# One core, RWKV attention into balanced experts: the threshold search on whole 16-bit distances, with its digits in partitions and its digit counts added up in PSUM

## The chip, the cores and the metric

One Trainium2 chip, one of its cores. The time is the device time of one execution, in microseconds (us); the kernel before has a median of 393.06 us over 3 runs (392.99 to 393.11).

## What is computed

The reference is an RWKV attention over `r, k, v` of 4 batches x 8 heads x 768 steps x 48 channels, whose output is regarded as 3072 tokens of 384 channels, and then a mixture of 8 experts with exactly balanced loads:

```python
logits = x @ w_gate                      # 3072 x 8
order = np.argsort(-logits.flatten())
for idx in order:                        # greedy, highest score first
    tok, e = idx // E, idx % E
    if assigned[tok] >= 0 or counts[e] >= cap:
        continue                         # cap = 3072 // 8 = 384
    assigned[tok] = e
    counts[e] += 1
for e in range(E):
    mask = assigned == e
    out[mask] = np.maximum(x[mask] @ w1[e], 0.0) @ w2[e]
```

`w1` is 384 x 1024 for each expert and `w2` 1024 x 384. The greedy loop can be done expert by expert: every free token proposes to its best open expert; the first expert that reaches 384 proposals, as a threshold on the score comes down, is full and closes with the tokens above the threshold, and the rest goes on without it. So seven searches for a threshold come one after another, and each also gives the 384 token numbers of one expert.

## The kernel before

It has three stretches. The **attention** (class `Mild`) fills about the first 125 us and writes the token rows to DRAM and the scores to `LG` (128 partitions x 24 tokens x 8 experts; called `ML` in the class `Assignment`). The **bridge** (to about 163 us) is written by hand under a fixed order: one expert, the "star", has its first 256 tokens (`EARLY`) chosen while attention still runs, and the matmuls of these (`x.early`, called piece by piece through `go(m)`) are laid between the steps of searches one and two. Then come the **experts** (`x.run`), whose matmuls are seven-product and fifteen-product schemes on half-size blocks (L1656, L1753, L1784) beside plain ones (L1679, L1811). There a scheduler orders the work: searches three to seven are a generator `later()`, and `due` in `x.run` pulls its next step at set parts of an expert's own work; the last argument of `x.run`, `{1: 5, 2: 7, 3: 8, 4: 8, 5: 7}`, says how many steps are pulled beside which expert.

A **search** is `likely_steps` (L1079). `m` (L1088) is each token's best open score, `prop` says which expert that is. Three times it divides the interval of thresholds by 16: `count` (L968 to L991) makes `ind` (128 partitions x 24 tokens x 16 candidate thresholds, 1 where the token's score reaches it), and three matmuls multiply it with `prop` (L980), eight tokens each, into `counts`. Of that 128x64 block only the diagonal of 8 blocks means anything, so VectorE (DVE) masks it (`own`), adds it up (`cnt`, L988), spreads the result over 16 digits (`wide`), and a fourth matmul with a matrix of ones (L991) gives every partition the 16 x 8 counts. From these DVE gets the digit `dg`, the next `cand` and `low` (L1103 to L1114); after the third digit also `fills`, `fmax` (the expert that closes) and `acc` (its tokens, L1132). Two matmuls (L1136, L1137) and a scan number the tokens; `tokens` then lists them (matmuls L1441, L1466), and GpSimd (POOL) gathers the rows with three indirect DMAs `xg` (L1557). `yield`s stand behind each count, each sum and the numbering, seven in a search.

`leave` (L1068 to L1073) closes the expert and the tokens: DVE builds a mask `dead` and a predicated copy puts a large negative number (`NEG`) into `LG`; POOL adds `acc` to `taken` and `fmax` to `last`. Before, `taken` is read only by the step for the last expert.

```python
tt(ind, self.by_token(m, ND), self.by_expert(cand), ALU.is_ge)                 # L968
tt(self.own[:, 0:G, :], each, self.same, ALU.mult)
nc.tensor.matmul(all_ps..., self.ones_h, wide..., start=True, stop=True)       # L991
nc.vector.copy_predicated(out=self.ML, mask=dead, data=self.neg...)            # L1071
```

Of the kernel before, what the change touches and what calls it, by code (L numbers as in the profile page):

```python
# [737 lines left out]
class Assignment:  # L738
# [24 lines left out]
    def __init__(self, ctx, tc, ML, CAP, C):  # L763
# [34 lines left out]
        new("digit_of_e", [128, ND, E], F16)  # L798
        new("digits", [128, ND], I32)
# [5 lines left out]
        new("cells", [128, 3, ND])  # L805
        new("cell", [128, 3])
# [20 lines left out]
    def constants(self):  # L827
# [39 lines left out]
        Q, NC = 128 // LO, self.CAP // 128  # L867
        nc.gpsimd.memset(self.quarter, 1.0)
        yield
        for sign, base in ((1, 0), (-1, LO - 1)):  # L870
# [10 lines left out]
        own = self.pool.tile([128, 2], I32, name="own_parts", bufs=1)  # L881
# [8 lines left out]
        yield  # L890
        nc.vector.tensor_scalar(out=self.turn, in0=self.iota[:, 0:Q], scalar1=self.own_turn, scalar2=None,
# [7 lines left out]
                                op0=ALU.mult, op1=ALU.add)  # L899
        yield  # L900
# [41 lines left out]
    def guess(self, ps, ident):  # L942

        nc, ND, most = self.nc, self.ND, self.most
        with ExitStack() as part:
            pool = part.enter_context(self.tc.tile_pool(name="guess", bufs=1))
            nc.tensor.matmul(ps, most.to_broadcast([128, 128]), ident, start=True, stop=True)
            nc.vector.tensor_reduce(out=self.value, in_=ps, axis=AX.X, op=ALU.max)
            nc.vector.tensor_single_scalar(out=self.value, in_=self.value, scalar=0.25, op=ALU.mult)
            rel = pool.tile([128, 3, ND], F32, name="rel")  # L950
            nc.vector.tensor_scalar(out=rel[:, 0, :], in0=self.digits, scalar1=1.0 / ND, scalar2=-1.0,
                                    op0=ALU.mult, op1=ALU.add)
            nc.vector.tensor_single_scalar(out=rel[:, 1, :], in_=self.digits, scalar=ND ** -2.0, op=ALU.mult)
            nc.vector.tensor_scalar(out=rel[:, 2, :], in0=self.digits, scalar1=-1.0, scalar2=ND ** -3.0,
                                    op0=ALU.add, op1=ALU.mult)
            nc.vector.tensor_scalar(out=self.cells, in0=rel, scalar1=self.value, scalar2=None, op0=ALU.mult)
            for g in range(3):
                nc.vector.tensor_single_scalar(out=self.cell[:, g:g + 1], in_=self.value,
                                               scalar=float(ND) ** -(g + 1), op=ALU.mult)
# [83 lines left out]
    def general_fill(self):  # L1043

        out = self.new_outs()
        with ExitStack() as part:
            pool = part.enter_context(self.tc.tile_pool(name="surely", bufs=1))
            self.surely(pool, **out)
        tok = self.tokens(out["place"])
        self.leave(out)  # L1050
        return out["fmax"], tok
# [10 lines left out]
    def leave(self, out):  # L1062

# [15 lines left out]
    def likely_steps(self, fmax, acc, place, on_fmax=None):  # L1079
        nc, ML, pool, ps, tt = self.nc, self.ML, self.pool, self.ps, self.tt  # L1080
        NT, E, ND, CAP = self.NT, self.E, self.ND, self.CAP
# [6 lines left out]
        nc.vector.tensor_reduce(out=m, in_=ML, axis=AX.X, op=ALU.max)  # L1088
# [3 lines left out]
        nc.vector.scalar_tensor_tensor(out=low, in0=self.cell[:, 0:1], scalar=float(-ND), in1=start,  # L1092
                                       op0=ALU.mult, op1=ALU.add)
        for g in range(3):
            all_ps = yield from self.count(pool, m, prop, cand, self.digit_of_e)
            if g == 0:
                eq = pool.tile([128, NT, E], F32, name="eq", bufs=1)
                tt(eq, prop, self.by_expert(self.first_e), ALU.mult)
                em = pool.tile([128, NT], F32, name="em")
                nc.vector.tensor_reduce(out=em, in_=eq, axis=AX.X, op=ALU.max)  # L1100
            if g < 2:
                base = pool.tile([128, ND], F32, name="base")
                nc.vector.tensor_scalar(out=base, in0=self.cells[:, g + 1, :], scalar1=low, scalar2=None, op0=ALU.add)  # L1103
                most = pool.tile([128, ND], F32, name="most")
                nc.vector.tensor_reduce(out=most, in_=all_ps, axis=AX.X, op=ALU.max)
                full = pool.tile([128, ND], F32, name="full")
                nc.vector.tensor_single_scalar(out=full, in_=most, scalar=float(CAP), op=ALU.is_ge)
                dg = pool.tile([128, 1], F32, name="dg")
                nc.vector.tensor_reduce(out=dg, in_=full, axis=AX.X, op=ALU.add)
                cand = pool.tile([128, ND], F32, name="cand")  # L1110
                nc.vector.scalar_tensor_tensor(out=cand, in0=self.cell[:, g:g + 1].to_broadcast([128, ND]), scalar=dg,
                                               in1=base, op0=ALU.mult, op1=ALU.add)
                was, low = low, pool.tile([128, 1], F32, name="low")
# [980 lines left out]
```

## Time and profile before

| | |
|---|---|
| median of the runs | 393.06 us |
| the profiled execution, its own time | 391.89 us |
| its span, from the first instruction to the last | 389.9 us |
| granted TensorE clock | 0.995 |
| TensorE (PE) busy | 371.9 us, 95% |
| VectorE (DVE) busy | 276.8 us, 71% |
| ScalarE (ACT) busy | 206.2 us, 53% |
| GpSimd (POOL) busy | 144.1 us, 37% |

In a row of the timeline stand the start, the time from the first start to the last end, the engine, the line, the operation with out<-in, for a matmul the tile of the array it uses (rows*columns), its shape and how many in a row; in brackets the idle time before it and what ended that. Ends of matmuls are modelled and overlap the next start, so what a matmul costs PE is read from start to start. An fp32 matmul is listed as two.

### The profile page before, as it was taken

The page shows a single profiled execution, that of the slowest core. Times are in us where ns is not written, and L with a number is a line of the kernel's source. Part 1 is how long each engine was busy: PE and PEld are TensorE (multiplying, and loading weights), DVE is VectorE, ACT ScalarE, POOL GpSimd, SP SyncE. Part 2 cuts the span into 40 slices and gives each one's busy share as a digit, 9 for nine tenths or more (in the row PEclk, how much of TensorE's full clock was granted, in tenths as well). Part 3 has the DMA queues.
Part 4 walks back from the last instruction along what each step waited for, and adds up shares of the span by engine and source line. Part 5 has one row for each costly group of instructions (what it writes and reads, how often), then busy time and mean ns, then how long its engine had stood idle before and what let it go on. Part 6 is the DMA issues. An engine that isn't in the chain of part 4 may idle for free. (4 is left out here: it accounts for less than half of the span.)

```text
span 389.9 us, 9804 instructions
## 1 busy us (share of the span) xinstructions
PE 371.9 (95%) x3720; PEld 301.0 (77%) x3720; DVE 276.8 (71%) x913; ACT 206.2 (53%) x545; POOL 144.1 (37%) x195
## 2 busy tenths in 40 slices
PE   8899999999999999999999999999999989989992
PEld 7777888888877766687577798558657779989991
DVE  6755768586885767977869939917867897994630
ACT  4897989888873311227228345423622734834620
POOL 7878979767742013022122121220330213070020
PEclk9999999999999999999999999999999999999998
DMA  7979878787593165551460470380190137190010
GB/s 146 198 151 206 194 171 178 158 179 163 108 361 83 44 218 206 185 202 43 184 220 22 148 276 23 92 334 0 49 381 16 41 130 275 34 356 20 2 62 27
DMA packets 95336, 57.36 MB, mean 147 GB/s; under 512 B 77232, under 2 KB 89520, under 8 KB 95280
## 3 DMA queue, kind: packets, MB, share of 16 engines
q1 hardware_dynamic: 91936, 47.21, 42.9%
q0 software_dynamic: 3104, 9.44, 6.8%
q8 instruction: 31, 0.51, 0.6%
q14 instruction: 25, 0.20, 0.2%
q10 hardware_dynamic: 240, 0.00, 0.0%
HBM read 47.20 MB, written 9.44 MB: 145 GB/s over the span
## 5 line engine op out<-in xcount | busy, mean ns | idle before, releaser
L1679 PE MATMUL h_ps<-xT,w 128*128 128x384 f32 (+1 forms) x264 | 71.3, 424 | 0.0
L496 ACT ACTIVATE AT<-ident,dd 128x128 f32<-128x128 f32 x192 | 59.7, 394 | 1.5 <-DVE dd L449 1.4
L1679 PEld LDWEIGHTS h_ps<-xT,w 128*128 128x128 f32 x264 | 42.8, 191 | 20.9 <-issue 0.8
L1805 POOL DMA_INDIRECT out_dram<-o_all,to x16 | 20.1, 1259 | 99.7 <-DVE cnt L988 26.0
L1557 POOL DMA_INDIRECT xg<-x_rows,tok x22 | 22.1, 1003 | 72.5 <-DVE parts L968 33.4
L1593 ACT COPY xT<-xq 32x288 f32<-32x288 f32 (+1 forms) x112 | 45.5, 406 | 3.4 <-DVE xq L1586 1.5
L1682 ACT ACTIVATE hid<-h_ps 128x384 f32<-128x384 f32 (+1 forms) x40 | 17.9, 447 | 53.4 <-PE h_ps L1679 49.9
L513 DVE COPY_PREDICATED AT<-mask,g_ps 64x512 f32<-64x512 uint8 (+1 forms) x48 | 32.4, 725 | 16.8 <-PE g_ps L506 14.5
L1811 PE MATMUL o_ps<-w,hid 128*128 128x384 f32 x96 | 34.5, 494 | 0.0
L506 PE MATMUL g_ps<-rT,kT 48*64 48x128 f32 (+1 forms) x768 | 26.3, 255 | 1.4 <-DVE AT L513 1.0
L437 POOL TENSOR_TENSOR kss<-krs,wk 128x384 f32<-128x384 f32 x24 | 24.4, 1016 | 8.1 <-DVE krs L341 4.6
L546 PE MATMUL y_ps<-AT,vts 128*64 128x128 f32 x384 | 25.7, 276 | 0.0
L444 POOL TENSOR_TENSOR rk<-rk,u_bc 128x384 f32<-128x384 f32 x24 | 24.1, 1004 | 1.9
L506 PEld LDWEIGHTS g_ps<-rT,kT 48*64 48x64 f32 x768 | 20.6, 132 | 5.1 <-issue 1.0
L443 POOL TENSOR_TENSOR rk<-krs 128x384 f32<-128x384 f32 x24 | 24.5, 1022 | 0.0
L1811 PEld LDWEIGHTS o_ps<-w,hid 128*128 128x128 f32 x96 | 17.1, 190 | 9.0 <-issue 1.5
L546 PEld LDWEIGHTS y_ps<-AT,vts 128*64 128x64 f32 x384 | 20.6, 137 | 1.0 <-issue 0.7
L1644 ACT ACTIVATE hid<-kept_P 128x384 f32<-128x384 f32 x18 | 9.4, 523 | 16.9 <-DVE kept_P L1648 16.5
L478 DVE TENSOR_TENSOR rT<-rT_ps,WR 112x512 f32<-112x512 f32 x23 | 15.7, 683 | 3.2 <-PE rT_ps L459 3.1
L565 ACT COPY x<-y_ps 128x512 f32<-128x512 f32 x24 | 14.1, 587 | 5.6 <-PE y_ps L546 4.5
L449 DVE TENSOR_REDUCE dd<-rk 128x8 f32<-128x384 f32 x24 | 13.0, 543 | 5.1 <-POOL rk L444 5.1
L459 PE MATMUL rT_ps<-ident,krs 128*112 128x128 f32 x96 | 15.7, 285 | 0.6 <-ACT krs L345 0.5
(351 smaller groups left out, 831.9 us busy)
## 6 DMA issues: line engine op xcount, KB each, us to landing
w<-in_moe_w_dram SPq DMA_DIRECT2D x18, 1536.0 KB, 9.1
krs<-in_k_dram SPq DMA_DIRECT2D x24, 192.0 KB, 3.6
krs<-in_r_dram SPq DMA_DIRECT2D x24, 192.0 KB, 3.6
vts<-in_v_dram SPq DMA_DIRECT2D x24, 192.0 KB, 3.7
x_rows<-xr SPq DMA_DIRECT2D x24, 192.0 KB, 2.7
xg<-x_rows,tok POOLq DMA_INDIRECT x22, 5.6
out_dram<-o_all,to POOLq DMA_INDIRECT x16, 2.8
out_dram<-o_sb,to POOLq DMA_INDIRECT x5, 6.3
```

The costliest lines, as they stand in the source:

```text
L437: self.nc.gpsimd.tensor_mul(self.kss[:, n % self.NS].rearrange("p (g h) d -> p g h d", g=2)[:, :, :, 0:D], src, self.wk.rearrange("p (g h) ...
L443: nc.gpsimd.tensor_mul(rk, self.krs[:, n % self.NK, 1, 0:H, 0:D], self.krs[:, n % self.NK, 0, 0:H, 0:D])
L444: nc.gpsimd.tensor_mul(rk, rk, self.u_bc)
L496: nc.scalar.mul(AT[:, z, a, :], self.ident, dd[:, h:h + 1])
L506: nc.tensor.matmul(g_ps[ts(i, PD), z, a, i * PD:], kT[rows, a, ts(i, PD)], rT[rows, a, i * PD:], start=True, stop=True)
L513: nc.vector.copy_predicated(out=AT[keys, :, :, steps], mask=mask, data=g_ps[keys, :, :, steps])
L546: nc.tensor.matmul(yv[q * PD:(q + 1) * PD, o // 2, o % 2, :], lhsT, rhs, start=(o // 2, q) not in seen, stop=stop, skip_group_check=True)
L1557: nc.gpsimd.indirect_dma_start(out=xg[:, c, :], out_offset=None, in_=x_dram[0:within, :], in_offset=bass.IndirectOffsetOnAxis(ap=tok[:, 0, ...
L1593: nc.scalar.copy(to[ts(q, 32), 0:nb, :, g, :], xq[ts(g, 32), 0:nb, :, q, :])
L1679: nc.tensor.matmul(h_ps[j][:, at], w1[:, f, ts(j, 128)], xT[:, f, at], start=(f == 0), stop=(f == KD - 1))
L1805: nc.gpsimd.indirect_dma_start(out=to, out_offset=bass.IndirectOffsetOnAxis(ap=tok, axis=0), in_=o_sb, in_offset=None)
L1811: nc.tensor.matmul(o_ps, hid[:, j, ts(c, 128)], w2[:, j, :], start=(j == 0), stop=(j == KF - 1))
```

## The change

- **Tables.** `own_slot`, `own_digit`, `same_slot`, `digit_cols`, `weight_of`, `step_of`, `first_e_h` are built with the other constants during attention (10 more steps, DVE and POOL).
- **Whole distances.** A search first works out `rel`: each token's distance below the start, in the smallest steps of the search, as int16 (L1127 to L1131). `m` gets `taken` times `NEG` added here (L1127), so a taken token drops out in `m` and not in `LG`. `ind` compares int16 with a constant table and is fp16.
- **Sums on PE, digits in partitions.** `per_slot` masks the counts, and a matmul with `digit_cols` (16 output rows, 72 columns, L1153) adds up the eight diagonal blocks with digits in 16 partitions. DVE reduces 16x72 to 16x8 (`cnt`), and decides `full`.
- **The digit, added up in PSUM.** A matmul of `weight_of` (16 rows) with `full` (one column, L1173) adds this digit, times 256, 16 or 1, to a column `digits` that every partition then reads; after the third digit another one of nine columns (L1172) gives `found`. `now` (L1143) is `rel` less the digits so far.
- **Leaving.** `leave` adds `NEG` to the column of the expert that closes. `early` no longer masks `LG` for its tokens.
- **Steps.** A search has ten `yield`s in place of seven, and the lists in the bridge and at `x.run` are adapted.

```diff
+        new("same_slot", [128, G, E])
+        new("digit_cols", [128, ND], F16)
+        new("weight_of", [ND, 3, 128], F16)
+        new("step_of", [128, 3, ND, 128 // self.LO], I16)
+        new("per_slot", [128, G + 1, E], F16)
...
+        nc.vector.tensor_scalar(out=self.same_slot, in0=self.iota[:, 0:G].unsqueeze(2).to_broadcast([128, G, E]),
+                                scalar1=self.own_slot, scalar2=None, op0=ALU.is_equal)
+        yield
+        nc.vector.tensor_scalar(out=self.digit_cols, in0=self.iota[:, 0:ND], scalar1=self.own_digit, scalar2=None,
+                                op0=ALU.is_equal)
+        yield
+        for g in range(3):
+            nc.gpsimd.memset(self.weight_of[:, g, :], float(ND ** (2 - g)))
+            yield
+            nc.gpsimd.iota(self.step_of[:, g], pattern=[[ND ** (2 - g), ND], [0, Q]],
+                           base=-ND ** 3 + (ND ** (2 - g) if g < 2 else 0), channel_multiplier=0)
+            yield
...
     def guess(self, ps, ident):
 
         nc, ND, most = self.nc, self.ND, self.most
...
+        nc.tensor.matmul(ps, most.to_broadcast([128, 128]), ident, start=True, stop=True)
+        nc.vector.tensor_reduce(out=self.value, in_=ps, axis=AX.X, op=ALU.max)
+        nc.vector.tensor_scalar(out=self.value, in0=self.value, scalar1=0.25, scalar2=1e-30, op0=ALU.mult, op1=ALU.max)
+        nc.vector.tensor_copy(self.span, self.value)
+        nc.vector.tensor_single_scalar(out=self.cell, in_=self.value, scalar=float(ND) ** -3, op=ALU.mult)
+        nc.vector.reciprocal(self.per_cell, self.cell)
...
     def leave(self, out):
+
+        nc, pool, tt = self.nc, self.pool, self.tt
+        fmax, acc = out["fmax"], out["acc"]
+        fe = pool.tile([128, self.E], F32, name="fe")
+        nc.vector.tensor_scalar(out=fe, in0=self.first_e, scalar1=fmax, scalar2=NEG, op0=ALU.is_equal, op1=ALU.mult)
+        tt(self.ML, self.ML, self.by_expert(fe), ALU.add)
+        nc.gpsimd.tensor_tensor(out=self.taken, in0=self.taken, in1=acc, op=ALU.add)
+        nc.gpsimd.tensor_tensor(out=self.last, in0=self.last, in1=fmax, op=ALU.add)
+
+    def leave_surely(self, out):
...
         i, self.fill = self.fill, self.fill + 1
         start, value, fills, upto = self.value, self.values[:, i:i + 1], self.fills[:, i, :], self.upto[:, ds(E - 2 - i, NT)]
         self.value = value
-        cand = pool.tile([128, ND], F32, name="cand")
-        nc.vector.tensor_scalar(out=cand, in0=self.cells[:, 0, :], scalar1=start, scalar2=None, op0=ALU.add)
+        low = pool.tile([128, 1], F32, name="low")
+        tt(low, start, self.span, ALU.subtract)
         m = pool.tile([128, NT], F32, name="m")
         nc.vector.tensor_reduce(out=m, in_=ML, axis=AX.X, op=ALU.max)
-        prop = pool.tile([128, NT, E], BF16, name="prop")
+        nc.vector.scalar_tensor_tensor(out=m, in0=self.taken, scalar=NEG, in1=m, op0=ALU.mult, op1=ALU.add)
+        off = pool.tile([128, NT], F32, name="off")
+        nc.vector.tensor_scalar(out=off, in0=m, scalar1=low, scalar2=start, op0=ALU.max, op1=ALU.subtract)
+        rel = pool.tile([128, NT], I16, name="rel")
+        nc.vector.tensor_scalar(out=rel, in0=off, scalar1=self.per_cell, scalar2=0.0, op0=ALU.mult, op1=ALU.min)
+        prop = pool.tile([128, NT, E], F16, name="prop")
         tt(prop, ML, self.by_token(m), ALU.is_equal)
-        low = pool.tile([128, 1], F32, name="low")
-        nc.vector.scalar_tensor_tensor(out=low, in0=self.cell[:, 0:1], scalar=float(-ND), in1=start,
-                                       op0=ALU.mult, op1=ALU.add)
+        bank = ps.tile([128, 512], F32, name="counts")
+        at = 3 * (2 * G + 1) * E
+        digits, found = bank[:, at:at + 1], bank[:, at + 1:at + 2 + E]
         for g in range(3):
-            all_ps = yield from self.count(pool, m, prop, cand, self.digit_of_e)
+            each = bank[:, ds(g * G * E, G * E)]
+            sums = bank[0:ND, ds(3 * G * E + g * (G + 1) * E, (G + 1) * E)]
+            now = rel
+            if g:
+                now = pool.tile([128, NT], I16, name="now")
+                nc.vector.tensor_scalar(out=now, in0=rel, scalar1=digits, scalar2=None, op0=ALU.subtract)
+            ind = pool.tile([128, NT // Q, ND, Q], F16, name="ind", bufs=1)
+            tt(ind, self.by_four(now, NT, ND), self.step_of[:, g].unsqueeze(1).to_broadcast([128, NT // Q, ND, Q]),
+               ALU.is_ge)
+            for j in range(NT // G):
+                nc.tensor.matmul(each, ind[:, ts(j, G // Q)].rearrange("p j d i -> p (j d i)"),
+                                 prop[:, ts(j, G), :].rearrange("p i e -> p (i e)"),
+                                 start=(g == 0 and j == 0), stop=(j == NT // G - 1), skip_group_check=True)
+            yield
+            tt(self.per_slot[:, 0:G, :], each.rearrange("p (i e) -> p i e", e=E), self.same_slot, ALU.mult)
+            nc.tensor.matmul(sums, self.digit_cols, self.per_slot.rearrange("p i e -> p (i e)"),
+                             start=False, stop=True, skip_group_check=True)
+            yield
             if g == 0:
-                eq = pool.tile([128, NT, E], F32, name="eq", bufs=1)
-                tt(eq, prop, self.by_expert(self.first_e), ALU.mult)
+                eq = pool.tile([128, NT, E], F16, name="eq", bufs=1)
+                tt(eq, prop, self.by_expert(self.first_e_h), ALU.mult)
                 em = pool.tile([128, NT], F32, name="em")
                 nc.vector.tensor_reduce(out=em, in_=eq, axis=AX.X, op=ALU.max)
+            cnt = pool.tile([ND, E], F32, name="cnt")
+            nc.vector.tensor_reduce(out=cnt, in_=sums.rearrange("p (i e) -> p e i", e=E), axis=AX.X, op=ALU.add)
+            full = pool.tile([ND, E + 1], F16, name="full")
             if g < 2:
...
-        nc.vector.scalar_tensor_tensor(out=fills, in0=dge, scalar=dg, in1=self.first_e,
+                most = pool.tile([ND, 1], F32, name="most")
+                nc.vector.tensor_reduce(out=most, in_=cnt, axis=AX.X, op=ALU.max)
+                nc.vector.tensor_single_scalar(out=full[:, E:E + 1], in_=most, scalar=float(CAP), op=ALU.is_ge)
+            else:
+                nc.vector.tensor_single_scalar(out=full[:, 0:E], in_=cnt, scalar=float(CAP), op=ALU.is_ge)
+                with nc.allow_low_precision(reason="whole numbers"):
+                    nc.vector.tensor_reduce(out=full[:, E:E + 1], in_=full[:, 0:E], axis=AX.X, op=ALU.max)
+                nc.tensor.matmul(found, self.weight_of[:, 2, :], full, start=False, stop=True, skip_group_check=True)
+            nc.tensor.matmul(digits, self.weight_of[:, g, :], full[:, E:E + 1], start=False, stop=True,
+                             skip_group_check=True)
+            yield
+
+        nc.vector.scalar_tensor_tensor(out=fills, in0=found[:, 0:E], scalar=found[:, E:E + 1], in1=self.first_e,
                                        op0=ALU.is_equal, op1=ALU.mult)
+        nc.vector.tensor_reduce(out=fmax, in_=fills, axis=AX.X, op=ALU.max)
         past = pool.tile([128, NT], F32, name="past")
-        nc.vector.tensor_scalar(out=past, in0=m, scalar1=value, scalar2=None, op0=ALU.is_ge)
-        nc.vector.tensor_reduce(out=fmax, in_=fills, axis=AX.X, op=ALU.max)
+        nc.vector.tensor_scalar(out=past, in0=rel, scalar1=digits, scalar2=-1.0 - ND ** 3, op0=ALU.subtract, op1=ALU.is_ge)
+        nc.vector.scalar_tensor_tensor(out=value, in0=digits, scalar=self.cell, in1=low, op0=ALU.mult, op1=ALU.add)
         nc.vector.scalar_tensor_tensor(out=acc, in0=em, scalar=fmax, in1=past, op0=ALU.is_equal, op1=ALU.mult)
...
-        dead = pool.tile([128, KB, E], U8, name="e_dead", bufs=1)
-        nc.vector.tensor_copy(dead, acc.unsqueeze(2).to_broadcast([128, KB, E]))
-        nc.vector.copy_predicated(out=ML[:, 0:KB, :], mask=dead,
-                                  data=self.neg.unsqueeze(2).to_broadcast([128, KB, E]))
         tt(self.taken[:, 0:KB], self.taken[:, 0:KB], acc, ALU.add)
-        nc.vector.tensor_scalar(out=self.own[:, self.G, :], in0=self.first_e, scalar1=self.star,
+        nc.vector.tensor_scalar(out=self.per_slot[:, self.G, :], in0=self.first_e, scalar1=self.star,
                                 scalar2=float(EARLY // self.G), op0=ALU.is_equal, op1=ALU.mult)
...
                 search = walk.likely_steps(**first, on_fmax=lambda fmax: have.update(v=x.load_weights(1, fmax)))
-                for m in (1, 5, 2, 5, 2, 6, 5):
+                for m in (2, 2, 2, 2, 2, 2, 2, 2, 3, 5):
                     next(search)
...
                 go(7)
+                next(search)
+                go(2)
                 next(search)
                 go(2)
                 next(search)
...
         x.run(ahead, later(), (a for a in [*out_rows[2:NT - 1], None]),
-              {1: 5, 2: 7, 3: 8, 4: 8, 5: 7}, xT)
+              {1: 7, 2: 10, 3: 11, 4: 11, 5: 10}, xT)
```

A digit of the third search beside the first expert's products, on PE. Before:

```order
L1753 MATMUL pa_ps<-w_2788,hid 128x192 x4
L980 LDWEIGHTS ind
L980 MATMUL counts<-prop,ind 128x64
L1753 MATMUL pc_ps<-w_2788,hid 128x192 x4
L1753 MATMUL pb_ps<-T_3116,S_3149 128x192 x4
L991 LDWEIGHTS ones_h
L991 MATMUL counts<-wide,ones_h 128x128
L1753 MATMUL pa_ps<-T_3118,S_3151 128x192 x4
```

Now (`per_slot`, `digit_cols`: the sums; `full`, `weight_of`: the digit):

```order
L1148 LDWEIGHTS ind
L1148 MATMUL counts<-prop,ind 128x64
L1800 MATMUL pa_ps<-w_2778,hid 128x192 x4
L1153 LDWEIGHTS digit_cols
L1153 MATMUL counts<-per_slot,digit_cols 16x72
L1800 MATMUL pc_ps<-w_2778,hid 128x192 x4
L1800 MATMUL pb_ps<-T_3089,S_3140 128x192 x4
L1173 LDWEIGHTS weight_of
L1173 MATMUL counts<-full,weight_of 128x1
L1800 MATMUL pa_ps<-T_3091,S_3142 128x192 x4
```

The stream of products is now left twice after each count and not once, both times for a small matmul. (The three counts read alike; one is shown.)

The start of the second search in the bridge, on DVE, before:

```order
L1068 TENSOR_SCALAR fe<-first_e,fmax 128x8
L968 TENSOR_TENSOR dead<-acc,fe 128x192
L1071 COPY_PREDICATED LG<-dead,neg 128x192
...
L1088 TENSOR_REDUCE m<-LG 128x24
L968 TENSOR_TENSOR prop<-LG,m 128x192
L1092 SCALAR_TENSOR_TENSOR low<-cell,values 128x1
L968 TENSOR_TENSOR ind<-m,cand 128x384
```

and now:

```order
L1094 TENSOR_SCALAR fe<-first_e,fmax 128x8
L995 TENSOR_TENSOR LG<-LG,fe 128x192
...
L1126 TENSOR_REDUCE m<-LG 128x24
L1127 SCALAR_TENSOR_TENSOR m<-taken,m 128x24
L1129 TENSOR_SCALAR off<-m,low,values 128x24
L1131 TENSOR_SCALAR rel<-off,per_cell 128x24
L995 TENSOR_TENSOR prop<-LG,m 128x192
L995 TENSOR_TENSOR ind<-rel,step_of 128x384
```

The new second row on `m` reads `taken`, which POOL writes; on POOL the order is as it was:

```order
L1604 DMA xg<-x_rows,tok 128x384
L1604 DMA xg<-x_rows,tok 128x384 x2
L1096 TENSOR_TENSOR taken<-taken,acc 128x24
L1097 TENSOR_TENSOR last<-last,fmax 128x1
L1852 DMA out_dram<-e_o_sb,to 3072x384
```

Nothing moved on POOL, but a row of DVE's search now needs one of its results, which stands behind three gathers.

More of the change, by code (lines that the diff above doesn't have):

```diff
@@ L803, in __init__ @@
         new("last", [128, 1])
-        new("cells", [128, 3, ND])
-        new("cell", [128, 3])
+        new("span", [128, 1])
+        new("cell", [128, 1])
+        new("per_cell", [128, 1])
         new("value", [128, 1])
@@ L867, in constants @@
         Q, NC = 128 // LO, self.CAP // 128
+        assert Q == 4 and G == 8 and ND == 16
         nc.gpsimd.memset(self.quarter, 1.0)
@@ L880, in constants @@
         yield
-        own = self.pool.tile([128, 2], I32, name="own_parts", bufs=1)
+        own = self.pool.tile([128, 5], I32, name="own_parts", bufs=1)
         nc.vector.tensor_single_scalar(out=own[:, 0:1], in_=self.own_i, scalar=Q.bit_length() - 1,
@@ L944, in guess @@
         nc, ND, most = self.nc, self.ND, self.most
[L945 to L951, printed above, removed]
-                                    op0=ALU.mult, op1=ALU.add)
[L953 to L959, printed above, removed]
+        nc.tensor.matmul(ps, most.to_broadcast([128, 128]), ident, start=True, stop=True)
[4 more added lines that the diff above has]
+        nc.vector.reciprocal(self.per_cell, self.cell)
     def by_token(self, t, n=None):
@@ L1049, in general_fill @@
         tok = self.tokens(out["place"])
-        self.leave(out)
+        self.leave_surely(out)
         return out["fmax"], tok
@@ L1101, in likely_steps @@
+            nc.vector.tensor_reduce(out=cnt, in_=sums.rearrange("p (i e) -> p e i", e=E), axis=AX.X, op=ALU.add)
+            full = pool.tile([ND, E + 1], F16, name="full")
             if g < 2:
[L1102 to L1112, printed above, removed]
@@ L1113, in likely_steps @@
-                was, low = low, pool.tile([128, 1], F32, name="low")
-                nc.vector.scalar_tensor_tensor(out=low, in0=self.cell[:, g:g + 1], scalar=dg, in1=was,
-                                               op0=ALU.mult, op1=ALU.add)
-        full = pool.tile([128, ND, E], F32, name="full_e")
-        nc.vector.tensor_single_scalar(out=full, in_=all_ps, scalar=float(CAP), op=ALU.is_ge)
-        dge = pool.tile([128, E], F32, name="dge")
-        nc.vector.tensor_reduce(out=dge, in_=full.rearrange("p d e -> p e d"), axis=AX.X, op=ALU.add)
@@ L1121, in likely_steps @@
-        dg = pool.tile([128, 1], F32, name="dg")
-        nc.vector.tensor_reduce(out=dg, in_=dge, axis=AX.X, op=ALU.max)
-        past_low = pool.tile([128, 1], F32, name="past_low")
-        tt(past_low, low, self.cell[:, 2:3], ALU.subtract)
-        nc.vector.scalar_tensor_tensor(out=value, in0=self.cell[:, 2:3], scalar=dg, in1=past_low,
-                                       op0=ALU.mult, op1=ALU.add)
-        nc.vector.scalar_tensor_tensor(out=fills, in0=dge, scalar=dg, in1=self.first_e,
+                most = pool.tile([ND, 1], F32, name="most")
```

21 lines of the change are left out of this document (19 added, 2 removed).

## The prediction

> **What bounds the kernel now.** I read the page's engine totals first, then busy time by stretch, then the timeline of PE beside the searches.
>
> ```profile
> PE 371.9 (95%) x3720; PEld 301.0 (77%) x3720; DVE 276.8 (71%) x913; ACT 206.2 (53%) x545; POOL 144.1 (37%) x195
> 126.00:163.00 37.00, 35.67 (x195) 25.50 (x194) 27.86 (x130) 9.42 (x23) 5.83 (x9) 1.00 0.43 146
> 163.00:383.00 220.00, 216.12 (x1214) 172.53 (x1212) 160.67 (x544) 96.75 (x228) 46.38 (x50) 1.00 0.38 134
> ```
>
> The columns of the two stretches are length, then busy time of PE, weight loads, DVE, ACT, POOL. The changed code runs in the bridge (126 to 163) and beside the experts (163 to 383). PE is idle for 37.00 - 35.67 = 1.3 us in the first and 220.00 - 216.12 = 3.9 us in the second. DVE has 160.67 of 220 us to do, so it has slack on the whole. The rule for what follows: a microsecond of extra PE work in these stretches is a microsecond at the end, and work taken from DVE is worth no more than those of the 5.2 idle microseconds that end on a search.
>
> How the searches stand in PE's stream (here the sixth search's first digit):
>
> ```profile
> 300.93 1.46 PE L1753 MATMUL pa_ps<-T,S 128*128 128x192 f32 x8
> 302.23 0.81 PE L1753 MATMUL pb_ps<-w,S 128*128 128x192 f32 x4
> 303.11 0.26 PE L980 MATMUL counts<-prop,ind 128*128 128x64 bf16 x3
> 303.21 0.90 PE L1753 MATMUL pb_ps<-w,S 128*128 128x192 f32 x4
> 303.94 1.14 PE L1753 MATMUL pa_ps<-T,S 128*128 128x192 f32 x6
> 305.07 0.22 PE L991 MATMUL counts<-wide,ones_h 128*128 128x128 f16 x1
> 305.13 0.54 PE L1753 MATMUL pa_ps<-T,S 128*128 128x192 f32 x2
> 305.50 0.81 PE L1811 MATMUL o_ps<-w,hid 128*128 128x384 f32 x2
> ```
>
> Undisturbed, eight 192-column products take 302.23 - 300.93 = 1.30 us, 0.1625 each. From 303.11 to 303.94 three counts and four products (0.65) take 0.83: the counts cost 0.18. From 305.07 to 305.50 the sum and two products (0.325) take 0.43: one lone small matmul costs 0.105, of which only 0.06 lies before the next start and 0.045 appears in the product behind it. All matmuls here use the 128*128 tile.
>
> **The change, part by part.** *DVE.* The groups of DVE from 122 us on (count | sum in us, mean in ns):
>
> ```profile
> L968 DVE TENSOR_TENSOR ind<-m,cand 128x384 bf16<-128x384 f32 x21 | 11.6, 551 | 0.0
> L968 DVE TENSOR_TENSOR wide<-digit_of_e,cnt 128x128 f16<-128x128 f16 x21 | 4.7, 223 | 0.5
> L968 DVE TENSOR_TENSOR row<-lo_of,lo 128x768 f16<-128x768 int16 x8 | 4.4, 550 | 0.0
> L968 DVE TENSOR_TENSOR oh<-hi_of,hi 128x288 f16<-128x288 int16 x7 | 2.1, 301 | 0.0
> L1071 DVE COPY_PREDICATED_SCALAR LG<-dead,neg 128x192 f32 x7 | 3.0, 424 | 0.0
> L1130 DVE TENSOR_SCALAR past<-m,values 128x24 f32<-128x24 f32 x7 | 1.6, 232 | 0.0
> ```
>
> The new `ind` reads int16 and writes fp16, as `oh` and `row` do; a line through these two (301 at 288, 550 at 768) gives 0.35 us at 384, 0.20 less than now. `wide` goes (0.22), three times in a search, and a predicated copy of 0.42 becomes an add. Five operations on 24 columns come in (`m` with `taken`, `off`, `rel`, two `now`), 0.23 each by `past`. Three times 0.20 and 0.22 against five times 0.23 is about even; with the mask, the `base`, `cand`, `low` and `dg` groups and `full_e` that also go, I estimate 2 to 3 us less per search. That DVE work is covered by PE's products now, so it is worth only the waits below. The ten new table steps run during attention, beside a PE that is the busiest engine there too: nothing.
>
> *More interruptions of PE.* Per search the three sums stay lone matmuls and three digits come in, the last of them with a second one behind it. Three times 0.105, and 0.03 for the second of a pair (313.92 to 313.95 below), is 0.345; for seven searches **+2.4 us**. Bounds: if a lone one with few rows or columns costs only those 0.03, seven of them (0.21) stand against today's three sums (0.315), -0.7 in all; if each new one costs as much as three counts, (3 x 0.18 + 0.03) x 7 = +4.0. I take the middle one, from the same kind of place and size.
>
> *Smaller tiles.* The new sums have 16 output rows, the digits are summed over 16 rows. In the attention part, weights of fewer rows or columns are listed with a smaller tile, and there changing tiles shows a price:
>
> ```profile
> 119.42 0.19 PE L1441 MATMUL e_some_ps<-e_vals,e_row 128*128 128x32 f16 x1
> 119.55 1.09 PE L546 MATMUL y_ps<-AT,vts 128*64 128x128 f32 x16
> 120.66 0.57 PE L597 MATMUL x_ps<-ident,x 112*128 112x112 f32 x4
> 121.07 0.18 PE L1466 MATMUL list_ps<-e_both,alike 128*128 128x24 f16 x1
> 121.10 0.58 PE L597 MATMUL x_ps<-ident,x 112*128 112x112 f32 x4
> 121.61 0.67 PE L546 MATMUL y_ps<-rT,states 48*64 48x128 f32 x16
> ```
>
> Four `x_ps` take 0.41 (120.66 to 121.07) when a full-size tile follows and 0.51 (121.10 to 121.61) when a 48*64 one does: 0.10 for leaving a stream of fp32. A small 16-bit matmul with a 128*64 one behind it holds PE for 0.13 (119.42 to 119.55), while between equal tiles the like takes 0.02 (313.95 to 313.97 below): 0.11 for going on in another tile. Together 0.21 for a switch out and back; of each side 0.045 is already in the 0.105 above, so 0.12 comes on top. Six switched places in a search (three sums, three digits, the pair counting once) times seven searches is 42: **+5.0 us**. Bounds: nothing, if 16 rows in the midst of 128 are no change of tile to the array; 42 x 0.21 = +8.8, if both sides are paid in full. I take the value between, which is nearer to the rows.
>
> The Trainium skill, on the page "TensorEngine Tiling (Array Packing)", section "Tiling Modes" (Key Properties), speaks against the change: "Changing tiling mode (not just tile) drains the TensorE". The 0.10 and 0.11 above agree with it. It has no price; if it didn't hold for these shapes, the sum would lose its 5.0 us.
>
> *The bridge.* The second search's `m` now waits for `taken`:
>
> ```profile
> 146.32 0.95 POOL L1557 DMA_INDIRECT xg<-x_rows,tok  x1 [0.30 <-DVE to L1484]
> 147.28 0.33 POOL L1072 TENSOR_TENSOR taken<-taken,acc 128x24 f32<-128x24 f32 x1
> 146.22 0.35 DVE L1088 TENSOR_REDUCE m<-LG 128x24 f32<-128x192 f32 x1
> 146.60 0.36 DVE L968 TENSOR_TENSOR prop<-LG,m 128x192 bf16<-128x192 f32 x1
> 142.92 4.76 PE L1932 MATMUL e_o_ps<-w,e_hid 128*128 128x384 f32 x14
> 147.59 0.26 PE L980 MATMUL counts<-prop,ind 128*128 128x64 bf16 x3
> 149.83 0.55 PE L1572 MATMUL xT_ps<-ident,xg 128*128 128x128 f32 x3 [0.55 <-DMA xg<-x_rows,tok]
> 153.31 0.22 PE L991 MATMUL counts<-wide,ones_h 128*128 128x128 f16 x1 [0.36 <-DVE wide L968]
> ```
>
> `taken` is the third gather's successor on POOL and ends at 147.61. Behind the waiting row on DVE stand `off`, `rel`, `prop`, `ind`; PE waits for these. Three times 0.23, 0.36 for `prop` and 0.35 for `ind` put the counts at 147.61 + 1.40 = 149.0. PE's cover, the same seven output products, is used up at 147.5: a new wait of about 1.5 us, where now there is none of note. Two smaller ones: the first search has three more rows of 0.23 ahead of a 0.20 shorter `ind` (about +0.4), and the second digit's sum stands straight behind its counts, with no product between, so it waits for `per_slot` (about +0.4). The later start takes away the gather's 0.55, and the shorter chain the 0.36. Together 1.5 + 0.8 - 0.9 = 1.4; some of it falls into PE's other short gaps, and I take **+1.2 us**. Bounds +0.3 (only the two small ones, less a wait) and +2.3 (nothing taken away).
>
> *Waits that go.* The waits of PE for a search beside the experts, and the largest that is not one:
>
> ```profile
> 215.13 0.22 PE L991 MATMUL counts<-wide,ones_h 128*128 128x128 f16 x1 [0.36 <-DVE wide L968]
> 217.96 0.17 PE L1136 MATMUL st_ps<-acc,ones 128*128 128x24 bf16 x1 [0.30 <-DVE acc L1132]
> 313.92 0.17 PE L1136 MATMUL st_ps<-acc,ones 128*128 128x24 bf16 x1 [0.40 <-DVE acc L1132]
> 313.95 0.17 PE L1137 MATMUL st_ps<-acc,rest_of 128*128 128x24 bf16 x1
> 313.97 1.22 PE L1656 MATMUL hc_ps<-xT,w 128*128 128x192 f32 x6
> 315.87 0.18 PE L1395 MATMUL st_ps<-sel,ones 128*128 128x48 bf16 x1 [0.67 <-DVE is_star L968]
> 351.01 0.92 PE L1656 MATMUL h_ps<-xT,w 128*128 128x192 f32 x4 [1.36 <-DVE kept_P L1648]
> ```
>
> The first two, 313.92 and 315.87 add up to 1.73 us, and the idle 3.9 less the 1.36 at 351.01, which is behind sums of products and stays, leaves 2.5 for all waits of the searches. The chain from counts to `acc` gets shorter and stands behind the same products, and `taken` now comes ahead of the scatter that holds `sel` up. I take **-2.0 us**, the four and part of the rest; bounds 0 (other DVE rows are in the way as before) and -2.5.
>
> *The sum:* 2.4 + 5.0 + 1.2 - 2.0 = +6.6 us. The profiled execution took 391.89, which becomes 398.5; the median of the runs stands 1.17 above that execution, so I predict **399.7 us**. All lower bounds give -2.9 (390.2), all upper ones +15.1 (408.2).
>
> **The rivals.** *(a) Tiles cost nothing.* The array takes 16 rows or columns like any small matmul; against it are the 0.10 and 0.11, for it that those rows come from long streams of other tiles and not from one lone matmul. 2.4 + 1.2 - 2.0 = +1.6: 394.7.
>
> *(b) The other side: faster.* The small matmuls are as cheap as the second of a pair, 0.03, since 16-column weights and one-column data leave no trace in the product behind, and tiles cost nothing; then the shorter DVE chain decides, at the waits quoted last. It gives -0.7 + 0.3 - 2.5 = -2.9: 390.2. It decides from a price of a new place, switch included, under 0.09 us: the 0.345 per search of the interruptions are three new places and one pair, and 42 places at 0.09, and seven seconds of a pair at 0.03, less the 21 sums of now at 0.105, are 1.8, which is about what the waits less the bridge give back (2.0 to 2.5, less 0.3 to 1.2). For it speaks that PE's idle time ends mostly on DVE; against it that even a 128-column lone sum costs 0.105 with no change of tile.
>
> *(c) Switches paid in full,* 0.21: 2.4 + 8.8 + 1.2 - 2.0 = +10.4: 403.5. It needs both drains on top of the interruption.
>
> *(d) The change doesn't find the right threshold:* with the distance rounded to whole steps a count might never be exactly 384, and the arm for unforeseen inputs would run attention anew, over 125 us more. The smallest step is a 4096th of the span, as before; I give it 0.01.
>
> **How the numbers follow.** Forecast 0.56, (a) 0.22, (b) 0.14, (c) 0.07, (d) 0.01. A measurement of this kernel can tell about 0.2% (0.8 us) from no change. Faster: nearly all of (b) and a little of (a), 0.15. Same: 0.06 of (a), some of (b) and of the forecast's lower edge, 0.11. Slower: the rest, 0.74. The likeliest case alone reaches from 396.5 to 402; the range goes down far enough to take in (a) and the upper part of (b), 392.0, and up to just short of (c), 402.8, which leaves out about 0.2.
>
> **What would show it.** In the changed profile: from the row of a lone sum or digit to the row behind the next products, 0.23 us more than the products take (0.105 and 0.12), and a tile other than 128*128 in its row; a wait of 1.0 to 1.5 us on PE at the second search's first counts, named after DVE, with DVE's `m` row starting when POOL's `taken` ends; no wait of PE for `acc` over 0.2 us beside the experts; PE busy in the expert stretch about 5 x 0.345 + 30 x 0.12 = 5.3 us more (five of the seven searches lie there). I am wrong if the switched rows are no dearer than 0.105 (then (a) or (b)), or if the bridge gets no longer.

## The result, and the profile after

The changed kernel takes 399.81 us (median; 399.49 to 400.01), the kernel before 393.02 us, four runs each: a ratio of 1.0172, 95% interval 1.0160 to 1.0184. It is 6.8 us slower; 399.7 us was predicted.

The page of the changed kernel, its span and engine totals, and then the two stretches of the prediction (length, busy time of PE, weight loads, DVE, ACT, POOL):

```profile
span 398.0 us, 9792 instructions
PE 380.4 (96%) x3748; PEld 303.3 (76%) x3748; DVE 258.5 (65%) x845; ACT 206.1 (52%) x545; POOL 144.1 (36%) x201
126.00:163.00 37.00, 34.78 (x196) 24.37 (x196) 18.74 (x95) 8.43 (x21) 5.60 (x9) 1.00 0.35 127
163.00:383.00 220.00, 218.10 (x1213) 171.48 (x1212) 151.79 (x509) 96.43 (x226) 44.28 (x49) 1.00 0.38 135
```

DVE lost 276.8 - 258.5 = 18.3 us of work, 2.6 us a search, as estimated, and the end came later all the same: PE gained 8.5 us of busy time for 28 more matmuls.

Where it went can be seen in one digit, the third search's first, beside the first expert's products:

```profile
174.40 0.25 PE L1148 MATMUL counts<-prop,ind 128*128 128x64 f16 x3
174.48 1.55 PE L1800 MATMUL pa_ps<-w,hid 128*128 128x192 f32 x8
175.96 0.20 PE L1153 MATMUL counts<-per_slot,digit_cols 128*16 128x72 f16 x1
176.09 1.57 PE L1800 MATMUL pc_ps<-w,hid 128*128 128x192 f32 x8
177.49 1.46 PE L1800 MATMUL pb_ps<-T,S 128*128 128x192 f32 x8
178.89 0.17 PE L1173 MATMUL counts<-full,weight_of 16*128 16x1 f16 x1
178.99 1.57 PE L1800 MATMUL pa_ps<-T,S 128*128 128x192 f32 x8
180.40 0.81 PE L1800 MATMUL pb_ps<-w,S 128*128 128x192 f32 x4
```

Eight undisturbed products take 1.30 us. The eight ahead of the digit take 178.89 - 177.49 = 1.40, the digit's own row 0.10, and the eight behind it 180.40 - 178.99 = 1.41: a matmul of one column holds PE for 0.31 us. The sum at 175.96 costs as much: 0.09 ahead (1.48, less 1.30, less the 0.09 that three counts leave behind), 0.13 itself, 0.10 behind. The tile columns read 128*16 and 16*128, where every other row here has 128*128. No engine is named in brackets: this is no wait, and the page's idle times don't show it.

In the bridge the new wait stands where it was expected. PE, POOL and DVE rows:

```profile
144.43 4.76 PE L1979 MATMUL e_o_ps<-w,e_hid 128*128 128x384 f32 x14
150.44 0.26 PE L1148 MATMUL counts<-prop,ind 128*128 128x64 f16 x3 [1.25 <-DVE ind L995]
153.73 0.55 PE L1619 MATMUL xT_ps<-ident,xg 128*128 128x128 f32 x3
156.63 0.19 PE L1153 MATMUL counts<-per_slot,digit_cols 128*16 128x72 f16 x1 [0.32 <-DVE per_slot L995]
148.79 0.24 POOL L1096 TENSOR_TENSOR taken<-taken,acc 128x24 f32<-128x24 f32 x1
149.06 0.18 DVE L1127 SCALAR_TENSOR_TENSOR m<-taken,m 128x24 f32<-128x24 f32 x1 [1.51 <-POOL taken L1096]
```

DVE's row waits 1.51 us for `taken`, PE 1.25 for the rows behind it. Against that, these are the largest of PE's bracketed waits from 126 us on, before and then after (sum, times, longest):

```profile
PE h_ps L1656 <- DVE kept_P L1648: 1.4, 1, 1.4
PE counts L991 <- DVE wide L968: 0.7, 2, 0.4
PE st_ps L1136 <- DVE acc L1132: 0.7, 2, 0.4
PE st_ps L1395 <- DVE is_star L968: 0.7, 1, 0.7
PE pa_ps L1753 <- ACT kept_P L1758: 0.6, 2, 0.4
```

```profile
PE counts L1148 <- DVE ind L995: 1.7, 2, 1.3
PE h_ps L1703 <- DVE kept_P L1695: 1.4, 1, 1.4
PE some_ps L1488 <- DVE vals L995: 0.5, 1, 0.5
PE counts L1153 <- DVE per_slot L995: 0.3, 1, 0.3
```

All four waits for a search beside the experts are gone (one of the two for `wide`, both for `acc`, and `is_star`), and so are those of products for ACT's `kept_P`. One new wait for a search has come there: 0.50 us for `vals`, at 227.77, ahead of the matmuls that list a search's tokens. The two for `ind` stand in the bridge, at the first counts of search one (0.41) and of search two (1.25).

**A ledger.** Both kernels issue the same 1245 product matmuls after attention. From the first transpose of the bridge (`e_xT_ps`) to the start of the last matmul I sum, start to start, what these take undisturbed (0.162 us for 192 columns, 0.323 for 384, 0.216 for 256, 0.112 for 128: 236.0 us in each kernel), and what each search matmul adds to the products around it (the commonest value of each kind); the rest are waits. The split between the last two rows is good to about 0.2 us, since it hangs on how the commonest value is taken.

| us | before | after | difference |
|---|---|---|---|
| the stretch | 256.1 | 263.1 | +7.0 |
| undisturbed products | 236.0 | 236.0 | 0 |
| search matmuls | 10.3 | 21.3 | +11.0 |
| waits | 9.8 | 5.8 | -4.0 |

The prices of one place: three counts 0.17, a lone sum 0.113 before and 0.328 after, a digit 0.303, the pair of the third digit 0.325, the numbering pair 0.136. The other 1.1 us by which the two spans differ lies in attention (the bridge starts at 126.41 before and 127.52 after). The runs show no steady effect of the change there: in the eleven experiments that keep its attention code and build its tables (some of them wider) the bridge starts anywhere from 125.96 to 127.47.

### The profile page after: what moved, and what is told of

It reads as the page before. It is cut to its first block, busy times and chain, and to the rows that moved or that the text cites. A ratio compares the mean times of both kernels' runs of the same rounds, so it can differ in the third digit from the quotient of the medians.

```text
span 398.0 us, 9792 instructions
## 1 busy us (share of the span) xinstructions
PE 380.4 (96%) x3748; PEld 303.3 (76%) x3748; DVE 258.5 (65%) x845; ACT 206.1 (52%) x545; POOL 144.1 (36%) x201
## 4 chain that ended last, share of the span: by engine, by line
PE 72%; issue 8%; DVE 7%; ACT 4%; DMA 3%; POOL 2%; another core or an unknown queue 1%; POOLq 0%; SPq 0%; DVEq 0%; ACTq 0%
PE h_ps L1726 16%; PE pa_ps L1800 7%; PE y_ps L546 6%; PE o_ps L1858 5%; PE g_ps L506 5%; PE pb_ps L1800 4%; PE h_ps L1703 3%; PE e_h_ps L1970 3%; PE kT_ps L459 3%; PE hb_ps L1703 2%; PE kv_ps L525 2%; ACT xT L1640 2%; PE x_ps L597 2%; PE rT_ps L459 2%; PE pc_ps L1800 2%
## 5 line engine op out<-in xcount | busy, mean ns | idle before, releaser
L1726 PE MATMUL h_ps<-xT,w 128*128 128x384 f32 (+1 forms) x264 | 72.3, 426 | 0.1
L1852 POOL DMA_INDIRECT out_dram<-o_all,to x16 | 18.9, 1180 | 113.1 <-DVE now L1143 36.8
L995 DVE TENSOR_TENSOR per_slot<-counts,same_slot 128x64 f16<-128x64 f32 x21 | 4.6, 218 | 20.4 <-PE counts L1148 20.4
L1800 PE MATMUL pa_ps<-T,S 128*128 128x192 f32 x80 | 16.8, 338 | 0.0
```

The lines of the kernel that those rows point to most:

```text
L1726: nc.tensor.matmul(h_ps[j][:, at], w1[:, f, ts(j, 128)], xT[:, f, at], start=(f == 0), stop=(f == KD - 1))
L1800: nc.tensor.matmul(ps, left[a][:, j, :], right[b][:, j, :], start=(j == 0 and name in ("P1", "P2", "P5")), stop=(j == KF // 2 - 1), skip_g ...
```

## The experiments

Theory: a change of tile drains the array, and this is the loss; the bridge adds a wait, and shorter DVE chains (rows of which each needs the one before) give back a part. Each run is compared with the kernel before on its own chip.

### Full tiles

Each partition p of 128 now holds the count of digit p mod 16, and each digit is summed from eight copies with an eighth of the weight. No operation is added.

```diff
-        new("digit_cols", [128, ND], F16)
-        new("weight_of", [ND, 3, 128], F16)
+        new("digit_cols", [128, G, ND], F16)
+        new("weight_of", [128, 3, 128], F16)
-            nc.gpsimd.memset(self.weight_of[:, g, :], float(ND ** (2 - g)))
+            nc.gpsimd.memset(self.weight_of[:, g, :], float(ND ** (2 - g)) / G)
-            sums = bank[0:ND, ds(3 * G * E + g * (G + 1) * E, (G + 1) * E)]
+            sums = bank[:, ds(3 * G * E + g * (G + 1) * E, (G + 1) * E)]
...
-            full = pool.tile([ND, E + 1], F16, name="full")
+            full = pool.tile([128, E + 1], F16, name="full")
```

> The changed kernel with the weights of the sums widened to 128 output rows (the 16 digit columns repeated eight times) and the digit matmuls summed over 128 rows with an eighth of the weight, so that each of these matmuls uses the whole array; their number, order and moving columns stay. Theory (a change of tile drains the array): in the changed kernel a sum costs PE 0.224 us beyond the products, a digit 0.199, the pair 0.222; they fall to about 0.057 and 0.05, the prices of the lone sum and the numbering pair in full tiles. That is 21 x 0.167 + 14 x 0.15 + 7 x 0.17 = 6.8 us less: 393.0. Rival (lone small matmuls are dear as such, whatever the tile): 399.8, as the changed kernel. Rival (waits on DVE take up what PE gains): 395 to 398, with new idle times of PE ahead of the sums and digits.

Measured: 391.61 us, ratio to the kernel before 0.9988 (0.9971 to 1.0004). The whole loss is gone. The same digit in this run:

```profile
171.21 1.55 PE L1801 MATMUL pa_ps<-w,hid 128*128 128x192 f32 x8
172.59 0.20 PE L1154 MATMUL counts<-per_slot,digit_cols 128*128 128x72 f16 x1
172.62 1.54 PE L1801 MATMUL pc_ps<-w,hid 128*128 128x192 f32 x8
174.00 1.46 PE L1801 MATMUL pb_ps<-T,S 128*128 128x192 f32 x8
175.30 0.17 PE L1174 MATMUL counts<-full,weight_of 128*128 128x1 f16 x1
175.33 1.55 PE L1801 MATMUL pa_ps<-T,S 128*128 128x192 f32 x8
176.71 0.81 PE L1801 MATMUL pb_ps<-w,S 128*128 128x192 f32 x4
```

Ahead of the digit nothing (175.30 - 174.00 = 1.30), 0.03 itself, 0.08 behind: 0.11 in place of 0.31. In the ledger the search matmuls fall from 21.3 to 12.8 and the waits rise from 5.8 to 6.7. The prices I gave in the expectation (0.224 and 0.057) end at the start of the next product and leave out what appears in that product (about 0.10 us behind a switch, 0.06 without one); the difference between them, 0.167, should have been 0.215. So the expected gain of 6.8 us was too small: the search matmuls gave 8.5, of which the waits took back 0.9.

### Only the sums in full tiles

The same, but `cnt` reads the first 16 rows of the sums and `full` and `weight_of` keep 16 rows.

> Only the sums widened to 128 output rows, the digits stay on 16 rows. Theory (each change of tile is paid where it stands, columns and rows alike): the sums fall from 0.224 to 0.057, the digits stay at 0.199: 21 x 0.167 = 3.5 us less, 396.3. Rival (only the 16-row side is dear, or only the 16-column side): 399.8, or all of the gain of the run with both, about 393.

Measured: 394.81 us, ratio 1.0075 (1.0056 to 1.0094). Sums 0.113, digits still 0.303: 4.5 us less than the changed kernel over the ledger's stretch, just what 21 sums at 0.215 make. Each switch is paid where it stands, by columns and by rows alike.

### Half the array, and three quarters

The same with 96 and with 64 rows in the sums and the digits (for 96 the last 32 rows of the digits have weight zero).

```diff
-        new("digit_cols", [128, ND], F16)
-        new("weight_of", [ND, 3, 128], F16)
+        new("digit_cols", [128, 6, ND], F16)
+        new("weight_of", [96, 3, 128], F16)
-            nc.gpsimd.memset(self.weight_of[:, g, :], float(ND ** (2 - g)))
+            nc.gpsimd.memset(self.weight_of[0:64, g, :], float(ND ** (2 - g)) / 4)
+            nc.gpsimd.memset(self.weight_of[64:96, g, :], 0.0)
```

> The changed kernel with the sums widened to 96 output rows and the digits summed over 96 rows (the last 32 with weight zero). Theory 1 (the price is for a change between shapes that the array is split into, and 96 no longer fits a half of it; in attention four transposes of 112 rows ran into a full-size matmul without a price): PE's price falls to 0.03 for a sum or digit, the time to that of full tiles, 391.6. Theory 2 (any matmul that leaves part of the array out pays): 0.2 each as before, 399.3. Between: only one of the two sides is gone, near 395.

> The same with 64 output rows and 64 rows summed over. Theory 1 (half of the array is still another shape): 0.2 us for each sum and digit stay, 399.3. Theory 3 (the price is for very few rows or columns, whose loading cannot overlap): it falls towards that of full tiles, 392 to 395.

Measured: 392.11 us, ratio 0.9995 (0.9985 to 1.0004) with 96; 399.31 us, ratio 1.0177 (1.0161 to 1.0194) with 64. With 96:

```profile
171.58 1.55 PE L1802 MATMUL pa_ps<-w,hid 128*128 128x192 f32 x8
172.97 0.20 PE L1155 MATMUL counts<-per_slot,digit_cols 128*96 128x72 f16 x1
173.00 1.54 PE L1802 MATMUL pc_ps<-w,hid 128*128 128x192 f32 x8
174.38 1.46 PE L1802 MATMUL pb_ps<-T,S 128*128 128x192 f32 x8
175.68 0.17 PE L1175 MATMUL counts<-full,weight_of 96*128 96x1 f16 x1
175.71 1.55 PE L1802 MATMUL pa_ps<-T,S 128*128 128x192 f32 x8
```

and with 64:

```profile
176.01 0.22 PE L1154 MATMUL counts<-per_slot,digit_cols 128*64 128x72 f16 x1
176.16 1.57 PE L1801 MATMUL pc_ps<-w,hid 128*128 128x192 f32 x8
177.56 1.46 PE L1801 MATMUL pb_ps<-T,S 128*128 128x192 f32 x8
178.96 0.17 PE L1174 MATMUL counts<-full,weight_of 64*128 64x1 f16 x1
179.06 1.24 PE L1801 MATMUL pa_ps<-T,S 128*128 128x192 f32 x6
```

96 rows or columns run as cheaply as 128 (0.11 a place), 64 as dearly as 16 (0.346 and 0.302). So it is neither that some of the array lies idle nor that the matmul is small: the price sets in between 96 and 64, and is paid for leaving the stream's tile and coming back. The Trainium skill ("TensorEngine Tiling (Array Packing)", "Tiling Modes", Key Properties) states that a change of tiling mode drains the TensorE. These runs agree with that, if 96 counts as the full mode, though no row shows the drain itself; here a round trip costs 0.19 to 0.23 us beyond the same matmul in a full tile.

### The taken tokens ahead of the gathers

```diff
+                walk.note(first)          # POOL: taken += acc, last += fmax
                 tok = walk.tokens(first["place"])
                 xg = x.gather(1, tok)
...
-                walk.leave(first)
+                walk.leave(first, noted=True)
```

> The changed kernel, but in the bridge POOL adds the first search's tokens to the taken ones ahead of the three gathers and not behind them. Theory: PE's wait of 1.25 us at the second search's first counts goes, DVE's row on the best scores no longer idles 1.51 us; some 0.3 comes back as a wait for the gathered rows, which now are needed earlier: 0.9 us less, 398.9. Rival (the gathered rows set the time there: all the gain comes back as a wait for them): within 0.2 of 399.8.

> Both: all new matmuls in full tiles, and the taken tokens added ahead of the gathers. Theory: the gains add up, 6.8 + 0.9 = 7.7 us: 392.1, just below the kernel before. Rival (the wait in the bridge only counts while PE is behind): as the run with full tiles alone, 393.

Measured: alone 397.33 us, ratio 1.0131 (1.0111 to 1.0151); with full tiles 390.01 us, ratio 0.9952 (0.9933 to 0.9970), faster than the kernel before. In the run alone, PE and DVE:

```profile
143.54 4.76 PE L1984 MATMUL e_o_ps<-w,e_hid 128*128 128x384 f32 x14
148.15 0.26 PE L1153 MATMUL counts<-prop,ind 128*128 128x64 f16 x3
151.44 0.55 PE L1624 MATMUL xT_ps<-ident,xg 128*128 128x128 f32 x3
146.77 0.18 DVE L1132 SCALAR_TENSOR_TENSOR m<-taken,m 128x24 f32<-128x24 f32 x1
```

From the start of the output products to the counts it is 4.61 us and was 6.01: 1.40 less. No wait for the gathered rows came in its place (`xT_ps` has no bracket): two more output products stand between the counts and them than before the change. Over the stretch the gain is 1.8 us alone (expected 0.9) and 1.4 with full tiles. The rival, that the gather sets the time, falls.

### The leaving step

The kernel with both repairs, but masking the scores as before (`dead`, predicated copy, `e_dead`), and `m` without `taken`:

> The kernel with full tiles and early taken tokens, but closing an expert writes the mask and the predicated copy into the scores again, and the taken tokens are not added to the best scores; the early tokens are masked as in the kernel before. Theory (PE's relief beside the experts is DVE's shorter work between the counts and the tokens, and most of that is in the search's steps): 0.4 us of DVE more for each search, mostly covered: 390.0 to 390.7. Rival (the relief comes from the leaving step): the 2 us come back, about 392.

And the other way round, the kernel before with only the leaving step of the change and its early `taken`:

> The kernel before with the leaving step of the change alone: the addend on the expert that closes, the taken tokens added to the best scores, and in the bridge added up ahead of the gathers; the search itself as before. Theory (as for the run with masks): within 0.7 us of the kernel before, since PE's waits stand behind the search's own chain. Rival (the leaving step is the relief): 2 us faster.

Measured: 390.44 us, ratio 0.9954 (0.9940 to 0.9968), the same as with the addend (0.9952); and 392.16 us, ratio 1.0002 (0.9993 to 1.0011). The leaving step does nothing measurable either way; in the ledger the waits are 5.4 and 5.5 us with and without it, and 10.0 where the search is the old one. The 4 us of relief are in the search's own steps.

### The search's chain, its load and its steps

Four variants of the kernel with both repairs. Longer chain: in the five searches beside the experts each `ind` is computed three times.

```diff
-            tt(ind, self.by_four(now, NT, ND), self.step_of[:, g]..., ALU.is_ge)
+            for _ in range(3 if i > 1 else 1):
+                tt(ind, self.by_four(now, NT, ND), self.step_of[:, g]..., ALU.is_ge)
```

> The kernel with full tiles and early taken tokens; in the five searches beside the experts each candidate table is computed three times over (same result), six more DVE operations of about 0.28 us a search, 1.7 us, each in the chain between a digit and the next counts. Theory (the relief is DVE's shorter chain under PE's products): waits of PE come back ahead of counts, sums and the numbering, 2 to 4 us in all: 392 to 394. Rival (the finer steps and the new order gave the relief, the products cover a longer chain as well): within 0.5 of 390.

More load off the chain: six such operations in `leave`, into a tile that nothing reads.

> The same six operations a search, but at its end, in the step that closes the expert, with nothing waiting for their results: the same load on DVE, off the chain from counts to tokens. Theory: the next counts have products enough ahead of them: 390 to 391. Rival (DVE's whole load counts, since sums of products queue behind whatever is ahead of them): as much as with the longer chain, 392 to 394.

Coarse steps: nothing is yielded behind a digit beside the experts, and `{1: 5, 2: 7, 3: 8, 4: 8, 5: 7}` steps are pulled; and the same with the longer chain.

```diff
-            yield
+            if i < 2:
+                yield
```

> The kernel with full tiles and early taken tokens, but the five searches beside the experts run in seven steps each as before the change (nothing is yielded behind a digit), with the old numbers of steps pulled. Theory (finer steps, and where the scheduler so puts the search's parts, gave the relief): waits of PE come back, 2 to 3 us: 392 to 393. Rival (the steps don't matter): within 0.5 of 390.

> Seven steps and the chain lengthened by the two extra candidate tables a digit together, 1.7 us a search. If the relief was the shorter chain under coarse steps (each hides the other's loss when alone): 3 to 4 us come back, 393 to 394, the waits of the kernel before. Rival (neither): 390 to 391.5, and the source of the relief stays open.

| | us | ratio to before, 95% interval | waits in the ledger |
|---|---|---|---|
| both repairs | 390.01 | 0.9952 (0.9933 to 0.9970) | 5.4 |
| longer chain | 391.87 | 0.9963 (0.9951 to 0.9975) | 6.4 |
| more load | 391.00 | 0.9942 (0.9922 to 0.9963) | 5.6 |
| coarse steps | 388.69 | 0.9920 (0.9892 to 0.9948) | 4.5 |
| coarse steps, longer chain | 390.86 | 0.9969 (0.9956 to 0.9982) | 6.0 |

The rows were taken on three chips, so their ratios compare and not their times. Load off the chain costs nothing measurable. The finer steps gave no relief: without them the time is the shortest of all, if anything (the intervals of the two runs overlap), and a wait of 0.8 us for `vals`, which the run with both repairs has, is gone. The chain counts, but less than expected: 1.7 us more in each of five searches brings back 1.0 us of waits with fine steps and 1.5 with coarse ones, not 2 to 4; with fine steps the two intervals overlap. PE's waits of the two runs with coarse steps, the shorter chain and then the longer:

```profile
PE counts L1159 <- DVE per_slot L996: 0.3, 1, 0.3
PE counts L1154 <- DVE ind L996: 0.3, 1, 0.3
```

```profile
PE counts L1155 <- DVE ind L996: 1.2, 3, 0.7
PE counts L1160 <- DVE per_slot L996: 0.3, 1, 0.3
```

The rest of the relief seems to be partly a matter of order. Of the kernel before, on ACT and PE:

```profile
238.93 3.07 ACT L1593 COPY xT<-xq 32x288 f32<-32x288 f32 x7
242.02 0.32 ACT L1758 COPY kept_P<-pa_ps 128x192 f32<-128x192 f32 x1
242.39 1.41 PE L1753 MATMUL pa_ps<-T,hid 128*128 128x192 f32 x7 [0.41 <-ACT kept_P L1758]
```

and ACT at the same place of the changed kernel:

```profile
246.22 2.19 ACT L1640 COPY xT<-xq 32x288 f32<-32x288 f32 x5
248.90 0.32 ACT L1805 COPY kept_P<-pa_ps 128x192 f32<-128x192 f32 x1 [0.48 <-PE pa_ps L1800]
```

Before, seven copies of gathered rows (`xT`) run ahead of the copy that PE waits for; now five, and the copy waits for PE. This place and its like at 274 us are worth 1.2 us in the ledger, and they go with the new search (the run with the old search and the new leaving step still has them). They seem to come from where the scheduler puts DVE's and ACT's rows rather than from the chain: with the longer chain none of them came back under coarse steps, and one of 0.2 us under fine ones. But no run changes this order alone, so it is read from the rows and not shown. How much of the 4 us each of the two causes makes was not settled.

## Why the prediction was right, and where it was not

The time came within 0.1 us. That is better than its steps.

- *PE is what bounds the kernel, and DVE's saved work is covered:* right in the main. 18.3 us less on DVE went with about 4 us less waiting of PE, and the stretch became 7.0 us longer.
- *More interruptions, +2.4 us:* right. With full tiles the search matmuls come to 12.8 us in the ledger, against 10.3 before: +2.5.
- *Smaller tiles, +5.0 us:* the mechanism was right and shown, the size was not. It measured 21.3 - 12.8 = 8.5 us, 0.20 a place and not 0.12. The step that failed is "of each side 0.045 is already in the 0.105 above". The rows of attention had given 0.21, the upper bound; the lone matmul's own 0.11 stays when the switch comes on top, so there was nothing to subtract.
- *The bridge, +1.2 us:* its parts were right, the sum too high. The wait for `taken` came (1.25; about 1.5 expected), as did the sum straight behind its counts (0.32), the later first counts, and the end of the gather's 0.55. The lag cannot be read at the list of the second search's tokens (`list_ps`, 165.30 before, 167.19 after), where the two kernels are at different products; at equal products (`h_ps` at 165.75 and 170.21) the lag is 4.46 us, 3.35 more than the 1.11 at its start. Two searches' matmuls are 2/7 of 11.0, 3.1; so waits changed by +0.2 us. Old short waits had gone too, and the transpose at the bridge's start, which had waited 0.42 for rows, took up half the lag that attention left.
- *Waits that go, -2.0 us:* too small, by about 2 us. Beside the experts the lag grows by 8.1 - 4.46 = 3.6 us while five searches' matmuls add 7.9: the waits fell by 4.2. The step that failed is the bound "the idle 3.9 less the 1.36 at 351.01 ... leaves 2.5 for all waits of the searches". A matmul's listed end lies 0.16 us behind the next possible start (eight products are listed as 1.46 us and take 1.30), so idle time by these ends misses the first 0.16 us of each wait and all of the shorter ones. Start to start, PE waited 9.8 us in that kernel from 126 us on, where its idle time said 5.2. The two waits for ACT were among them, which I had not counted as the search's.

So 3.5 us too few for the tiles stood against 3.2 us too many left in waits. That the total fell on the point is luck; that it was slower, and by what, is not: rival (a) was ruled out by the runs with 128, 96 and 64 rows, rival (b) needed a price under 0.09 and met 0.31, and rival (c) had the right price for the switch without the relief that went with it.

## What to carry to other kernels

A small matmul that stepped out of the stream's tile size cost the stream 0.19 to 0.23 us here, on both sides of it, and the profile books this as busy time; when the data were repeated or padded so that the small matmul used 96 or 128 rows and columns of the array, the price was gone. Read PE's waits from start to start against an undisturbed run of the same products, since idle time by modelled ends understates them, about twofold in the kernel before. Before a value is read on a critical chain, look at what stands ahead of its producer in that engine's queue: moving two POOL additions ahead of three gathers was worth 1.4 to 1.8 us here.

## What the runs showed of the hardware that was not expected

- The price of a smaller tile sets in between 96 and 64: 96 rows or columns cost 0.11 us a place like 128, and 64 cost 0.30 to 0.35, nearly as 16 (0.30 to 0.33).
- One column or 72, the price of a switched place is nearly the same (0.303 and 0.328), and so is that of an unswitched one (0.11). Most of an unswitched place, 0.08 us, appears in the fp32 products behind it and not in its own row (0.03).
- The execution of attention, over nearly the same code, ended up to 1.6 us apart in the profiled executions (bridge starts of 125.96 to 127.52). Differences of this size between two spans have to be located by stretch before they are explained.
